# Rebuilding the linear-attention half of a fused attention kernel, and giving its scheduler a model of side-by-side row tiles

## The chip, the cores and the metric

The kernel runs on one core of a Trainium2 chip. The time is the duration of one execution on the device in microseconds (us). Times below are medians of several executions; a ratio is the mean time of one kernel's fast runs over that of the other's fast runs of the same rounds, so it is not quite the ratio of the medians quoted beside it. Each run also reports the share of the full TensorE clock that was granted. Runs that took over 1.5% more than the fastest of their kernel in the same job are called slow and are left out of means and ratios.

## The reference

The program computes two independent attention layers on sequences of 2048 rows, with model width 512 and 32 heads of 16, and puts their outputs side by side.

```python
# A: softmax attention, 32 query heads share one key head and one value head
q = (x @ wq) as (32, 2048, 16);  k = x @ wk;  v = x @ wv        # k, v: (2048, 16)
a = concat_heads(softmax(q @ k.T / 4) @ v) @ wo
# B: linear attention, per head
q, k, v = split(x @ wqkv)
phi(u) = [softmax(u @ w_phi), softmax(-(u @ w_phi))]            # 16 + 16 features
kv = phi(k).T @ v;   z = sum over rows of phi(k)
b = concat_heads(phi(q) @ kv / (phi(q) @ z + 1e-6)) @ wo
out = concat([a, b], axis=-1)
```

## The kernel before

Part A is a stream of 2048 score tiles, each 128 keys by 512 queries of one head. A score matmul needs only 16 of its 32 rows of weights, so four heads sit on four row tiles (partitions 0, 32, 64, 96) of TensorE. Each tile has to be exponentiated. ACT does that for two or three tiles in one instruction (`L1616` in the profile). DVE does it with a bit trick: it writes the bits of a float16 with one multiply-add from PSUM (`L1708`), makes three shifted copies for four tiles at once (`L1721`), and PE sums the four with weights (`L1746`). Four such tiles are called a group here.

A list scheduler, written in Python and run while the program is built, decides how many groups DVE takes and in which order everything is issued. It keeps a clock for each engine; B's work is spread between A's. The order is fixed before the chip sees it (a check at the end falls back to a general version for inputs out of range; these inputs do not need it). The parts that the argument touches:

```python
def issue(self, j, start):              # the scheduler books job j on its engine
    dur = j.dur
    if j.eng == "pe" and j.mode != self.mode:
        dur += self.SWITCH              # changing between full, row and column tiling
        self.mode = j.mode
    self.te[j.eng] = start + dur        # PE is taken until then, whatever row tile it was
    ...

def next_dq(self):                      # offers the next score tile of a DVE group
    ...
    g = next((x for x in self.dleft if x not in self.busy), self.dleft[0])   # its row tile
    ...
    self.job(("dq", k), "pe", 0.22, scores, mode="row", nb=1, prio=1.0, ok=self.dq_ok)

# in run(): put matmuls on zeros ("fills") into a gap of PE, to keep its clock up
gap = s - te - ...
if n >= 2 and te > 14 and self.active(s) < self.ACTIVE:
    ...
```

B works row by row: project q and k transposed, copy them out of PSUM, multiply by `w_phi`, exponentiate into float32, normalise each feature, and only then use it:

```python
# per 128 rows, 32 times (16 for keys, 16 for queries)
ssum = reduce_add(epn, per head and sign)               # L1976, DVE
bmx = max(ssum, bmx);  rs = 1 / ssum                    # L1982, L1983, DVE
phi = epn * rs                                          # L1991, DVE, 128x1024
# keys: kv += phi.T @ [v, 1]
# queries: transpose phi on PE, copy out, multiply by kv and z, divide
den = ps[..., 64:68] + 1e-6;  rden = 1 / den            # L2067, L2069, DVE
o_sb = ps[..., 0:64] * rden                             # L2070, DVE
# transpose o, copy out, multiply by wo, copy out, store
```

## Time and profile before

The median was 853.77 us when the prediction was made (847.48 to 860.23). The profiled run took 863.85 us at a clock of 0.925. The first lines come from the profile page of the kernel before: the span, the busy time of each engine with its share of the span and its number of instructions, the granted clock in 40 slices (in tenths), and the chain of work that ended last, by engine.

```profile
span 862.1 us, 17064 instructions
## 1 busy us (share of the span) xinstructions
PE 785.0 (91%) x7214; PEld 252.0 (29%) x7278; DVE 728.3 (84%) x1286; ACT 777.2 (90%) x714; POOL 14.7 (2%) x46
...
## 2 busy tenths in 40 slices
...
PEclk9779979889999999998999999978979999699998
...
## 4 chain that ended last, share of the span: by engine, by line
DVE 53%; PE 30%; ACT 12%; DMA 2%; issue 2%; SPq 1%; DVEq 0%; POOL 0%; POOLq 0%
```

Three engines are close together: PE 91%, ACT 90%, DVE 84%. The clock row has five slices at 7 and one at 6. The next lines are groups of instructions by line of the kernel; after the bar stand busy us and mean ns of one, then the idle time of the engine just before them and what ended it.

```profile
## 5 line engine op out<-in xcount | busy, mean ns | idle before, releaser
L1616 ACT ACTIVATE f_PT<-f_ps 128x1536 bf16<-128x1536 f32 (+1 forms) x645 | 747.7, 1263 | 65.4 <-PE f_ps L1561 60.1
L1561 PE MATMUL f_ps<-f_QA,f_KR 32*128 32x512 bf16 x2048 | 348.9, 407 | 35.6 <-ACT f_PT L1616 11.8
L1708 DVE TENSOR_SCALAR f_Z<-f_ps 128x512 int16<-128x512 f32 x436 | 283.3, 679 | 41.3 <-PE f_ps L1561 39.9
L1721 DVE TENSOR_SCALAR f_Z<-f_Z 128x2048 int16<-128x2048 int16 x327 | 213.2, 681 | 0.9
...
L1378 PE MATMUL f_ps<-f_ones,f_zero 128*128 128x512 bf16 (+7 forms) x274 | 84.6, 385 | 2.1 <-POOL f_zero L1397 1.3
...
L1976 DVE TENSOR_REDUCE f_ssum<-f_epn 128x64 f32<-128x1024 f32 x32 | 38.6, 1205 | 2.6 <-ACT f_epn L1970 2.6
L1991 DVE TENSOR_TENSOR f_phi<-f_epn,f_rs 128x1024 bf16<-128x1024 f32 x32 | 38.7, 1210 | 0.1
```

ACT had 1612 tiles (2048 less 436) in 747.7 us, 0.464 us each. DVE had 436 tiles, 109 groups, in 283.3 + 213.2 us, 4.56 us per group. `L1378` are the fills. ACT waited 60.1 us for score matmuls. `L1976` and `L1991` are two of the linear part's DVE instructions; all of the linear part's DVE groups add up to about 194 us.

Two lines of the timeline of the kernel before (start us, duration us, engine, instruction) show what row tiles do on the chip:

```profile
start us, us, engine line op out<-in xcount [idle before <-releaser]
...
830.91 0.38 PE L1561 MATMUL f_ps<-f_QA,f_KR 32*128 32x512 bf16 x1
...
833.84 0.39 PE L1561 MATMUL f_ps<-f_QA,f_KR 32*128 32x512 bf16 x3
```

One score matmul keeps PE busy for 0.38 us, three on different row tiles for 0.39 us. The Trainium skill says the same in "TensorE: Matmul & The Clock Gate", Part 3 on packing: matmuls on different row groups run concurrently. The scheduler knew it for the two or three tiles that it issues as one job for ACT, but not for the single tiles it issues for DVE: each of those took 0.22 us of its PE clock even when it ran beside others.

### The profile page before, as it was taken

The page shows a single profiled execution, that of the slowest core. Times are in us where ns is not written, and L with a number is a line of the kernel's source. Part 1 is how long each engine was busy: PE and PEld are TensorE (multiplying, and loading weights), DVE is VectorE, ACT ScalarE, POOL GpSimd, SP SyncE. Part 2 cuts the span into 40 slices and gives each one's busy share as a digit, 9 for nine tenths or more (in the row PEclk, how much of TensorE's full clock was granted, in tenths as well). Part 3 has the DMA queues.
Part 4 walks back from the last instruction along what each step waited for, and adds up shares of the span by engine and source line. Part 5 has one row for each costly group of instructions (what it writes and reads, how often), then busy time and mean ns, then how long its engine had stood idle before and what let it go on. Part 6 is the DMA issues. An engine that isn't in the chain of part 4 may idle for free.

```text
span 862.1 us, 17064 instructions
## 1 busy us (share of the span) xinstructions
PE 785.0 (91%) x7214; PEld 252.0 (29%) x7278; DVE 728.3 (84%) x1286; ACT 777.2 (90%) x714; POOL 14.7 (2%) x46
## 2 busy tenths in 40 slices
PE   8989999999999999999899888999999999998894
PEld 2222223223323333322233333332333332222231
DVE  4778989998956999989996889998989778799942
ACT  4879989999999999999999999989899999799972
POOL 5000000000000000001000000000000000000000
PEclk9779979889999999998999999978979999699998
DMA  6841001111101111100111101110111110111110
GB/s 127 182 44 8 5 5 8 7 8 8 8 7 27 8 8 8 8 4 6 8 7 30 22 8 13 20 13 8 13 13 21 20 27 19 7 8 7 7 8 28
DMA packets 40922, 17.08 MB, mean 20 GB/s; under 512 B 32836, under 2 KB 38468, under 8 KB 40840
## 3 DMA queue, kind: packets, MB, share of 16 engines
q1 hardware_dynamic: 40840, 15.93, 14.8%
q8 instruction: 59, 0.97, 0.5%
q14 instruction: 23, 0.19, 0.1%
HBM read 3.19 MB, written 4.19 MB: 9 GB/s over the span
## 4 chain that ended last, share of the span: by engine, by line
DVE 53%; PE 30%; ACT 12%; DMA 2%; issue 2%; SPq 1%; DVEq 0%; POOL 0%; POOLq 0%
DVE f_Z L1708 18%; DVE f_Z L1721 14%; ACT f_PT L1616 12%; PE f_ps L1561 11%; PE f_ps L1658 5%; PE f_ps L1746 5%; DVE f_phi L1991 3%; DVE f_ssum L1976 3%; PE f_ps L1378 3%; PE f_ps L1929 2%; DVE f_accS L1384 2%; DVE f_o_sb L2070 1%; DVE f_rs L1983 1%; PE f_ps L1802 1%; DVE f_On L1789 1%
## 5 line engine op out<-in xcount | busy, mean ns | idle before, releaser
L1616 ACT ACTIVATE f_PT<-f_ps 128x1536 bf16<-128x1536 f32 (+1 forms) x645 | 747.7, 1263 | 65.4 <-PE f_ps L1561 60.1
L1561 PE MATMUL f_ps<-f_QA,f_KR 32*128 32x512 bf16 x2048 | 348.9, 407 | 35.6 <-ACT f_PT L1616 11.8
L1708 DVE TENSOR_SCALAR f_Z<-f_ps 128x512 int16<-128x512 f32 x436 | 283.3, 679 | 41.3 <-PE f_ps L1561 39.9
L1721 DVE TENSOR_SCALAR f_Z<-f_Z 128x2048 int16<-128x2048 int16 x327 | 213.2, 681 | 0.9
L1658 PE MATMUL f_ps<-f_PT,f_VA 128*32 128x512 bf16 x1612 | 169.3, 411 | 2.9 <-DVE f_accS L1384 2.8
L1561 PEld LDWEIGHTS f_ps<-f_QA,f_KR 32*128 32x128 bf16 x2048 | 82.9, 92 | 273.6 <-ACT f_PT L1616 100.7
L1746 PE MATMUL f_ps<-f_Z,f_VK 128*32 128x512 f16 x1744 | 123.6, 407 | 4.7 <-DVE f_Z L1721 2.1
L1378 PE MATMUL f_ps<-f_ones,f_zero 128*128 128x512 bf16 (+7 forms) x274 | 84.6, 385 | 2.1 <-POOL f_zero L1397 1.3
L1658 PEld LDWEIGHTS f_ps<-f_PT,f_VA 128*32 128x32 bf16 x1612 | 41.5, 93 | 120.1 <-issue 107.0
L1746 PEld LDWEIGHTS f_ps<-f_Z,f_VK 128*32 128x32 bf16 x1744 | 40.1, 100 | 61.6 <-issue 18.5
L1976 DVE TENSOR_REDUCE f_ssum<-f_epn 128x64 f32<-128x1024 f32 x32 | 38.6, 1205 | 2.6 <-ACT f_epn L1970 2.6
L1991 DVE TENSOR_TENSOR f_phi<-f_epn,f_rs 128x1024 bf16<-128x1024 f32 x32 | 38.7, 1210 | 0.1
L1929 PE MATMUL f_ps<-f_BxT,f_Bw 128*128 128x512 bf16 x111 | 33.3, 420 | 4.4 <-issue 2.3
L1970 ACT ACTIVATE f_epn<-f_ps 128x512 f32<-128x512 f32 x64 | 35.5, 626 | 1.8 <-PE f_ps L1961 1.6
L1378 PEld LDWEIGHTS f_ps<-f_ones,f_zero 128*128 128x128 bf16 (+2 forms) x274 | 21.4, 100 | 41.2 <-issue 28.9
L1384 DVE CAST f_qkT<-f_ps 128x512 bf16<-128x512 f32 x32 | 21.9, 685 | 9.7 <-PE f_ps L1929 9.5
L1789 DVE TENSOR_TENSOR f_On<-f_accS,f_denS 128x512 bf16<-128x512 f32 x31 | 21.1, 681 | 4.3 <-DMA f_denS<-f_denS 4.2
L1802 PE MATMUL f_ps<-f_wo_pad,f_On 128*128 128x512 bf16 x87 | 22.9, 381 | 2.1 <-issue 1.0
L1384 DVE COPY f_accS<-f_ps 128x512 f32<-128x512 f32 x31 | 21.1, 682 | 4.0 <-PE f_ps L1658 3.0
L1384 DVE CAST f_outA<-f_ps 128x512 bf16<-128x512 f32 x12 | 8.3, 690 | 18.5 <-PE f_ps L1802 18.5
L1513 DVE TENSOR_SCALAR f_KR<-f_ps,f_half 128x512 bf16<-128x512 f32 x8 | 5.6, 745 | 15.2 <-PE f_ps L1505 15.2
L1983 DVE RECIPROCAL f_rs<-f_ssum 128x64 f32<-128x64 f32 x32 | 17.4, 544 | 0.0
(83 smaller groups left out, 326.2 us busy)
## 6 DMA issues: line engine op xcount, KB each, us to landing
f_denS<-f_denS SPq DMA_DIRECT2D x124, 30.0 KB, 3.1
out_dram<-f_outB SPq DMA_DIRECT2D x16, 128.0 KB, 1.7
f_denC<-f_accS SPq DMA_DIRECT2D x124, 2.0 KB, 1.7
f_denS<-f_denC SPq DMA_DIRECT2D x124, 2.0 KB, 1.7
f_Bw<-in_B_wqkv_dram SPq DMA_DIRECT2D x1, 1536.0 KB, 7.4
out_dram<-f_outA SPq DMA_DIRECT2D x6, 256.0 KB, 2.3
f_wq<-in_A_wq_dram SPq DMA_DIRECT2D x1, 512.0 KB, 4.0
f_Bwo<-in_B_wo_dram SPq DMA_DIRECT2D x1, 512.0 KB, 10.1
```

The source lines that it names most:

```text
L1378: mm = pe.matmul(ps[0:m, bank, 0:n].rearrange("p (a n) -> p a n", n=128), lhsT=zero[0:r, 0:m], rhs=rhs, start=start, stop=start, **kw)
L1384: self.add("dve", lambda v: v.tensor_copy(out=out, in_=in_), reads=reads, writes=writes)
L1561: return pe.matmul(self.ps[:, bank, :], lhsT=self.KR[32 * g:32 * g + 32, sc % 2, kap * 128:(kap + 1) * 128], rhs=self.QA[32 * g:32 * g + 3 ...
L1616: self.add("act", lambda a: a.activation(out=PT[:, sl[0]:sl[0] + size, :], in_=ps[:, b0:b0 + size, :], func=ACT.Exp), reads=[("PS", b0 + i ...
L1658: mm = pe.matmul(ps[32 * g:32 * g + 32, bank, :], lhsT=w, rhs=PT[:, slots[g], :], start=start, stop=stop, tile_position=(0, 32 * g))
L1708: self.add("dve", lambda v: v.tensor_scalar(out=o, in0=ps[:, bank, :], scalar1=self.Z1, scalar2=self.Z0, op0=ALU.mult, op1=ALU.add), reads ...
L1721: self.add("dve", lambda v: v.tensor_scalar(out=Z[:, t], in0=Z[:, 0], scalar1=256.0 * t, scalar2=None, op0=ALU.add), reads=zk, writes=[("Z ...
L1746: mm = pe.matmul(ps[32 * g:32 * g + 32, bank, :], lhsT=w[:, k, :], rhs=Zf[:, k, sl[g], :], start=start and k == 0, stop=stop and k == 3, t ...
L1929: mm = pe.matmul(ps[:, bank, :], lhsT=w[:, dc, col0:col0 + 128], rhs=xT[:, dc, sck * 512:(sck + 1) * 512], start=(dc == 0), stop=(dc == 3))
L1970: self.add("act", (lambda a, sg: (lambda e: e.activation(out=epn[:, a, :], in_=ps[:, bank, :], func=ACT.Exp, scale=sg)))(a, sg), reads=[(" ...
L1976: self.add("dve", lambda v: v.tensor_reduce(out=ssum[:, r, :], in_=epn.rearrange("p a (h f) -> p (a h) f", h=32), axis=AX.X, op=ALU.add), ...
L1991: self.add("dve", lambda g: g.tensor_tensor(out=o, in0=i0, in1=i1, op=ALU.mult), reads=["epn", "epn2", ("rs", r)], writes=[("phi", pr)])
```

## The change

The linear part is rebuilt to use less DVE time. `wk @ w_phi` and `wq @ w_phi` are multiplied once on the chip, so features come straight from x. The key features stay unnormalised; the values are multiplied by the reciprocal sums instead, half as many rows of work as before. The query features are computed already transposed, for both signs, are never normalised, and their sums enter through a small matmul and one weight per head, sign and row.

```diff
+mm = pe.matmul(ps[...], lhsT=wT[:, 4 * w + c, ...], rhs=wphi[:, c, :], ...)   # fuse weights, once
-phi = epn * rs                        # 32 times 128x1024
+vS[:, :, :, 0:16] = v3 * rs           # 16 times 128x1024, keys only
+vS[:, :, :, 16:17] = rs
-tr: pe.transpose(phi)  ->  copy       # queries: transpose after the exponent
+b_pq: matmul(lhsT=Wq (both signs), rhs=xT), 512 columns;  ET = exp(ps)   # features on partitions
+b_qs: 32 small matmuls per 512 rows give both sums of each head; b_qw: weights from them
+o_sb[:, a] = ps[:, a] * w             # 32 times 128x512, both signs, added by the transpose on PE
```

The scheduler gets a clock for each row tile:

```diff
-        self.te[j.eng] = start + dur
+        if j.mode == "row" and j.name[0] in ("qk", "dq"):
+            ...
+            self.row_free = start + dur - j.dur + 0.02
+            for x in tiles:
+                self.tile_end[x] = start + dur
+        self.te[j.eng] = max(self.te[j.eng], start + dur)
...
+    def pe_from(self, j, te):          # from when PE can take j
+        if j.mode != "row" or self.mode != "row" or j.name[0] not in ("qk", "dq"):
+            return te
+        tiles = [self.dq_tile(self.row_free)] if j.name[0] == "dq" else self.row_tiles[j.name[1]]
+        return max([self.row_free] + [self.tile_end[g] for g in tiles])
```

And settings move: the ring of exponentiated tiles `RING` from 15 to 20, `HIGH` from 9 to 13 (how far value matmuls may lag), `AGE` from 5 to 3, the fill threshold `ACTIVE` from 5.8 to 6.4, the end of the stretch for B from 700 to 600. Fills may now also use a free PSUM bank, and some output buffers and the last output products are laid out anew.

## The prediction

> **What bounds the kernel now.** The work is one pool of 2048 score tiles (32 sub-rows x 512), exponentiated either by ACT or, by a bit trick, by DVE in groups of four. The page's busy table shows PE 91%, ACT 90% (777 us), DVE 84% (728 us) of the 862.1 us span. The groups by line give 1612 tiles to ACT (747.7 us, 0.464 us each) and 436 = 109 groups of four to DVE (283.3 + 213.2 us, 4.56 us per group). The rest of DVE, about 232 us, is copies and the linear part. So ACT and DVE together are the bound and PE is close behind; DVE time taken from the linear part is worth something only because the list scheduler refills it with score tiles. The chain that ended last agrees: DVE 53%, PE 30%, ACT 12%.
>
> **DVE removed (groups by form).** Linear part before: sums 38.6, phi 38.7, reciprocal 17.4, running max 6.8, q/k copies 21.9, v 10.8, transposed phi 10.9, den/rden/o 26.7, oT 6.5, outB 10.9, kv 4.7: about 194 us.
> **DVE added (estimates from the same durations).** Weight copies 12 x 0.68 = 8; key sums 16 x 1.2 = 19; reciprocal and max 16 x 0.76 = 12; values divided by sums 16 x 1.4 = 22; kv adds 7; query weights 4 x 2.9 = 11.5; scaled outputs 32 x 0.68 = 22; oT and outB 22: about 124 us. The skill page "VectorE: DVE Perf Modes" (perf-mode tier table) has tensor_reduce at 1x only, so bf16 features do not make the sum cheaper than the 1.205 us of now. Net saving about 70 us, 65 after overlap.
> **ACT:** 64 exps of 128x512 before and after (35.5 us): no change.
> **PE:** projections grow from 128 to 192 matmuls of 512 columns (+14 us), kv and transposes about even; each group moved to DVE needs 16 instead of 4 value matmuls (about +0.65 us). PE gets about 20-25 us more real work, but 84.6 us of it now are clock-keeping fills on zeros, so most is absorbed.
>
> **Critical share.** A balance: ACT busy share x T = 29.5 + 0.464 x (2048 - 4n), DVE share x T = other + 4.556 n, n groups. It returns 862 for before. With other = 165 and unchanged shares (90.1%, 84.5%) T = 841 (-2.5%). So of 65 us about 21 reach the time.
> **Scheduler.** Idle before ACT exps is 65 us (60 from score matmuls), before DVE's first step 41 us (40 likewise). In the timeline three row tiles take 0.39 us, as one does; the skill page "TensorE: Matmul & The Clock Gate" (Part 3, packing) says disjoint row groups run concurrently. The old model books 0.22 us of PE for each. With the new one and a ring of 20 instead of 15 I expect ACT near 91.5%, DVE near 87%: another 10-20 us. The tail (about 30 us after 830 with ACT half idle) shrinks by 1-3 us. Clock: 0.925 granted, but ACT is busy 91% in slow and in full-clock windows alike, so more fills buy little.
>
> Predicted: **824 us**, range 803 to 846; faster by over 2%: 0.76, within 2%: 0.20, slower: 0.04.
>
> **Right if:** DVE's linear lines sum to 115-135 us; DVE groups rise from 109 to 116-128 and ACT tiles fall to about 1540-1585; ACT's wait on score matmuls falls below 50 us; DVE busy stays 84-89%.
> **Wrong if:** DVE goes idle instead of taking groups, because banks are held longer (values wait for the sums in PSUM, four query-weight banks) or PE cannot feed it: then DVE falls below 82%, groups stay near 109 and time stays within 2%. Or PE saturates (over 95%). If the row-tile model alone removes most waits, time may be below 805.

## The result, and the profile after

The changed kernel took 814.96 us (809.98 to 815.92, 4 runs) beside 852.72 us of the kernel before (4 runs). The ratio is 0.9566 with a 95% interval of 0.9511 to 0.9621. One of the four runs of the kernel before, 860.23 us, is slow and not in the ratio. Predicted were 824 us with a range of 803 to 846. The same lines of the page after:

```profile
span 806.9 us, 17313 instructions
## 1 busy us (share of the span) xinstructions
PE 733.9 (91%) x7345; PEld 243.7 (30%) x7420; DVE 722.3 (90%) x1254; ACT 748.5 (93%) x690; POOL 16.7 (2%) x49
...
PEclk9788999999999999999999998999999999999997
...
## 4 chain that ended last, share of the span: by engine, by line
DVE 63%; PE 25%; DMA 5%; ACT 2%; SPq 2%; issue 2%; DVEq 0%
```

```profile
L1653 ACT ACTIVATE f_PT<-f_ps 128x1536 bf16<-128x1536 f32 (+1 forms) x621 | 721.4, 1264 | 45.3 <-PE f_ps L1598 42.1
L1745 DVE TENSOR_SCALAR f_Z<-f_ps 128x512 int16<-128x512 f32 x496 | 324.1, 682 | 34.9 <-PE f_ps L1598 34.3
L1598 PE MATMUL f_ps<-f_QA,f_KR 32*128 32x512 bf16 x2048 | 315.6, 390 | 31.1 <-DVE f_Z L1745 20.8
L1758 DVE TENSOR_SCALAR f_Z<-f_Z 128x2048 int16<-128x2048 int16 x372 | 244.5, 685 | 0.7
...
L1404 PE MATMUL f_ps<-f_ones,f_zero 128*128 128x512 bf16 (+7 forms) x204 | 61.2, 361 | 2.1 <-POOL f_zero L1423 1.3
...
L2152 DVE TENSOR_TENSOR f_Wk<-f_ps,f_wq 128x512 bf16<-128x512 f32 x32 | 21.9, 684 | 3.0 <-PE f_ps L2141 2.9
...
L2041 DVE TENSOR_TENSOR f_vS<-f_ps,f_rs 128x1024 bf16<-128x1024 f32 x16 | 19.5, 1220 | 1.2 <-PE f_ps L2031 1.1
...
L2015 DVE TENSOR_REDUCE f_ssum<-f_Ek 128x64 f32<-128x1024 bf16 x16 | 19.4, 1214 | 0.1
```

The groups of four on DVE rose from 109 to 124 (496 tiles), ACT's tiles fell from 1612 to 1552, its wait for score matmuls from 60.1 to 42.1 us, and its busy time from 777.2 to 748.5 us. Of the 55.2 us between the two profiled spans, 28.7 us are less work of ACT and 26.5 us less idle time of ACT. The 60 tiles that moved, at 0.464 us each, explain the first part: 27.8 us. The second part is smaller in usual runs: the trace before is of a slow run and the trace after of the fastest of its kernel, and the means of the fast runs (below) are only 41.8 us apart, which leaves about 14 us for it. The clock row is full almost everywhere. The windows from 60 to 760 us, first before and then after, give busy us (and instructions) of PE, PEld, DVE, ACT and POOL, then the granted clock, the DMA share and GB/s:

```profile
60.00:760.00 700.00, 648.87 (x6046) 212.09 (x6104) 618.58 (x1090) 658.30 (x609) 3.86 (x9) 0.93 0.12 12
```

```profile
60.00:760.00 700.00, 652.16 (x6648) 219.18 (x6716) 663.56 (x1140) 680.95 (x630) 4.83 (x10) 0.99 0.13 12
```

ACT went from 94.0% to 97.3% busy in this stretch, DVE from 88.4% to 94.8%, and the clock from 0.93 to 0.99.

### The profile page after: what moved, and what is told of

Read it like the earlier page. It is cut to its first block, busy times and chain, and to the rows that moved or that the text cites. A ratio compares the mean times of both kernels' runs of the same rounds, so it can differ in the third digit from the quotient of the medians.

```text
span 806.9 us, 17313 instructions
## 1 busy us (share of the span) xinstructions
PE 733.9 (91%) x7345; PEld 243.7 (30%) x7420; DVE 722.3 (90%) x1254; ACT 748.5 (93%) x690; POOL 16.7 (2%) x49
## 4 chain that ended last, share of the span: by engine, by line
DVE 63%; PE 25%; DMA 5%; ACT 2%; SPq 2%; issue 2%; DVEq 0%
DVE f_Z L1745 27%; DVE f_Z L1758 19%; PE f_ps L1598 8%; PE f_ps L1783 5%; PE f_ps L1695 4%; DMA f_AxT<-in_A_x_dram 2%; DVE f_vS L2041 2%; PE f_ps L2092 2%; ACT f_PT L1653 2%; DVE f_ssum L2015 2%; DVE f_accS L1410 2%; DMA f_BxT<-in_B_x_dram 2%; DVE f_On L1826 2%; PE f_ps L1839 2%; DVE f_Wk L2152 2%
## 5 line engine op out<-in xcount | busy, mean ns | idle before, releaser
L1653 ACT ACTIVATE f_PT<-f_ps 128x1536 bf16<-128x1536 f32 (+1 forms) x621 | 721.4, 1264 | 45.3 <-PE f_ps L1598 42.1
L1745 DVE TENSOR_SCALAR f_Z<-f_ps 128x512 int16<-128x512 f32 x496 | 324.1, 682 | 34.9 <-PE f_ps L1598 34.3
L1598 PE MATMUL f_ps<-f_QA,f_KR 32*128 32x512 bf16 x2048 | 315.6, 390 | 31.1 <-DVE f_Z L1745 20.8
L1758 DVE TENSOR_SCALAR f_Z<-f_Z 128x2048 int16<-128x2048 int16 x372 | 244.5, 685 | 0.7
L1404 PE MATMUL f_ps<-f_ones,f_zero 128*128 128x512 bf16 (+7 forms) x204 | 61.2, 361 | 2.1 <-POOL f_zero L1423 1.3
L2092 PE MATMUL f_ps<-f_BxT,f_Wq 128*128 128x512 bf16 x112 | 29.4, 380 | 3.3 <-issue 1.6
L2152 DVE TENSOR_TENSOR f_Wk<-f_ps,f_wq 128x512 bf16<-128x512 f32 x32 | 21.9, 684 | 3.0 <-PE f_ps L2141 2.9
L2041 DVE TENSOR_TENSOR f_vS<-f_ps,f_rs 128x1024 bf16<-128x1024 f32 x16 | 19.5, 1220 | 1.2 <-PE f_ps L2031 1.1
L2099 ACT ACTIVATE f_ET<-f_ps 128x512 bf16<-128x512 f32 x32 | 20.2, 636 | 0.4 <-PE f_ps L2092 0.4
L2015 DVE TENSOR_REDUCE f_ssum<-f_Ek 128x64 f32<-128x1024 bf16 x16 | 19.4, 1214 | 0.1
```

The costliest lines, as they stand in the source:

```text
L1404: mm = pe.matmul(ps[0:m, bank, 0:n].rearrange("p (a n) -> p a n", n=128), lhsT=zero[0:r, 0:m], rhs=rhs, start=start, stop=start, **kw)
L1598: return pe.matmul(self.ps[:, bank, :], lhsT=self.KR[32 * g:32 * g + 32, sc % 2, kap * 128:(kap + 1) * 128], rhs=self.QA[32 * g:32 * g + 3 ...
L1653: self.add("act", lambda a: a.activation(out=PT[:, sl[0]:sl[0] + size, :], in_=ps[:, b0:b0 + size, :], func=ACT.Exp), reads=[("PS", b0 + i ...
L1745: self.add("dve", lambda v: v.tensor_scalar(out=o, in0=ps[:, bank, :], scalar1=self.Z1, scalar2=self.Z0, op0=ALU.mult, op1=ALU.add), reads ...
L1758: self.add("dve", lambda v: v.tensor_scalar(out=Z[:, t], in0=Z[:, 0], scalar1=256.0 * t, scalar2=None, op0=ALU.add), reads=zk, writes=[("Z ...
L2092: mm = pe.matmul(ps[:, bank, :], lhsT=w[:, dc].rearrange("p x h a f -> p (x h a f)")[:, G * 128:G * 128 + 128], rhs=xT[:, dc, m * 512:(m + ...
```

## The experiments

Twelve kernels were run, four at a time on one chip beside the kernel before, with five rounds each. All gave correct results. "Clock" is the mean of the fast runs. The kernel before took 855.9 us on average over 24 fast runs of these three jobs, at a mean clock of 0.943. The changed kernel in its own job: 814.1 us over five runs, clock 0.969.

| run | linear part | row model | settings | groups | mean us | ratio (95%) | clock |
|---|---|---|---|---|---|---|---|
| before | old | old | old | 109 | 855.9 | 1 | 0.943 |
| e1 | old | new | old | 115 | 838.8 | 0.982 (0.976 to 0.988) | 0.965 |
| e2 | new | old | old | 109 | 838.9 | 0.980 (0.972 to 0.987) | 0.960 |
| e3 | new | old | new | 113 | 826.8 | 0.971 (0.964 to 0.978) | 0.967 |
| e4 | new | new | old | 121 | 828.4 | 0.971 (0.966 to 0.976) | 0.964 |
| after | new | new | new | 124 | 814.1 | 0.957 (0.951 to 0.962) | 0.969 |
| e5 | new, 70 us DVE added | new | new | 116 | 832.7 | 0.970 (0.967 to 0.974) | 0.964 |
| e6 | new | new | new, no fills | 123 | 823.8 | 0.960 (0.956 to 0.963) | 0.926 |
| e7 | old | old | old, more fills | 111 | 850.8 | 0.991 (0.987 to 0.996) | 0.952 |
| e8 | new | new | new, AGE 3.1 | 121 | 815.4 | 0.950 (0.947 to 0.954) | 0.976 |
| e9 | new | new | new, ring 15 | 124 | 813.4 | 0.949 (0.945 to 0.953) | 0.968 |
| e10 | old | old | searched | 114 | 845.1 | 0.987 (0.981 to 0.993) | 0.955 |
| e11 | new | new | searched | 125 | 808.1 | 0.943 (0.939 to 0.947) | 0.978 |
| e12 | new, A's products on POOL | new | searched | 125 | 827.9 | 0.965 (0.960 to 0.969) | 0.954 |

The changed kernel has 0.957 in its own job, and 0.949 in e9, whose instructions come in the same order. Ratios of different jobs are therefore good to about 0.8%; differences below are taken inside a job where they can be.

### e1 to e4: the parts one by one

e1 is the kernel before with the scheduler's diff above and nothing else. e2 is the changed kernel with that diff and the settings undone; "linear part new" in the table therefore also holds the other edits of the change (fills in free banks, output buffers and their order), which no run takes apart:

```diff
-        tiles = [...]                      # e2, e3: pe_from
-        return max([self.row_free] + ...)
+        return te
-        self.te[j.eng] = max(self.te[j.eng], start + dur)
+        self.te[j.eng] = start + dur
-    RING = 20;  HIGH = 13;  AGE = 3.0;  ACTIVE = 6.4;  T_B = (54.0, 600.0)     # e2, e4
+    RING = 15;  HIGH = 9;  AGE = 5.0;  ACTIVE = 5.8;  T_B = (54.0, 700.0)
```

> Kernel before with only the scheduler's new row-tile model; linear part, ring of 15 and settings as before. The program built has 115 DVE groups (before: 109). Theory 1 (mine: two gains that add, linear rebuild about -2.5% and scheduler with its settings -1 to -2.5%): 0.980 to 0.990 of before. Theory 2 (the two need each other; DVE is already 84% busy with the old linear part, so the better model alone finds little free DVE time): 0.985 to 1.00. ACT's wait on score matmuls falls from 60 us under both.

> New linear part with the old row-tile model and the old settings (ring 15, HIGH 9, AGE 5, ACTIVE 5.8, linear part spread to 700). Theory 1: the freed 65 us of DVE are refilled with score groups, about 118 groups, 0.975 of before. Theory 2: the old model books PE time for each score tile that the chip does not spend, so the scheduler does not offer the freed DVE time to score groups; the built program has 109 groups as before, DVE busy falls to about 660 us (80%), and the time falls only by what shorter waits give: 0.985 to 1.00.

> The changed kernel with the old row-tile model, new settings kept (built: 113 groups instead of 124). Theory 1: 0.965 to 0.975 of before (loses 1 to 2%). Theory 2: 0.975 to 0.99 of before, DVE busy about 670 us, so most of the gain is gone though DVE's linear work is as small as in the changed kernel.

> The changed kernel with its settings back (ring 15, HIGH 9, AGE 5, ACTIVE 5.8, linear part to 700), row-tile model and linear part new (built: 121 groups). Both theories: small loss against the changed kernel, 0.960 to 0.975 of before. If settings were the main thing: above 0.98.

Each part alone gave about 16 us in this job (854.6 us before): e1 0.982, e2 0.980. Added to the other, each gave about 10 us more (e4: 828.4), and the settings another 12 to 14 (e2 to e3; e4 to the changed kernel, across jobs). So the three add up, nearly. The rival, that the two need each other, fits the times less well: e1, e2 and e3 lie below its ranges (0.985 to 1.00 for the first two, 0.975 to 0.99 for e3), though all three intervals just reach into them. But its mechanism was half right. The page of e2, where the linear part alone is new:

```profile
span 841.0 us, 16959 instructions
...
PE 774.4 (92%) x7249; PEld 243.8 (29%) x7249; DVE 669.9 (80%) x1149; ACT 774.3 (92%) x714; POOL 16.3 (2%) x49
...
L1653 ACT ACTIVATE f_PT<-f_ps 128x1536 bf16<-128x1536 f32 (+1 forms) x645 | 748.2, 1275 | 53.0 <-PE f_ps L1597 50.0
...
L1745 DVE TENSOR_SCALAR f_Z<-f_ps 128x512 int16<-128x512 f32 x436 | 285.5, 684 | 69.0 <-PE f_ps L1597 67.9
```

No group moved: still 436 tiles on DVE, DVE fell to 80% busy as the rival said, and DVE's wait for score matmuls rose to 67.9 us. Yet ACT's waits fell: ACT is idle for 66.7 us (841.0 less 774.3), 84.9 before. So freed DVE time seems to pay without being refilled. In the table of waits of e2, the two PE queues together wait for DVE 147 us, 185 us before (sums of all such lines): PE, whose program is one fixed order, stands less long before instructions that need DVE, and so reaches ACT's score matmuls earlier (its waits for ACT rose from 121 to 139 us). That is a reading of the waits, not shown by a run of its own. The clock is a rival for much of it: from 60 us to 40 us before the end, the stretches of half clock that begin there add up to 51 us in e2 and to 102 us in the trace before. At the price found below, 23 us for 99 us, that is about 12 of the 18 us; by the mean clocks of this job (0.947 and 0.960), and 3.6 us per 0.01, it is about 5 of the 16 us.

### e5: 70 us of DVE work put back

```diff
+for i in range(58):
+    fn = lambda: self.add("dve", lambda v: v.tensor_reduce(out=scr, in_=src, axis=AX.X, op=ALU.add), ...)
+    self.job(("xx", i), "dve", 1.14, fn, prio=1.9, rel=70.0 + 11.0 * i)
```

> The changed kernel plus 58 useless DVE sums of 1.2 us (70 us, about what the linear rebuild saved), known to the scheduler, spread over 70 to 700 us, writing a scratch tile. The program built has 116 groups instead of 124. Theory 1 (the linear rebuild pays through DVE time that is refilled with score groups; the balance of the prediction gives 22 us for 70 us of DVE): 0.978 to 0.988 of before. Rival (it pays through fewer PSUM bank turns and shorter chains, not through DVE time): 0.957 to 0.968, nearly the changed kernel.

The measured ratio, 0.970, lies between both ranges, because the changed kernel itself was better in this job (0.950 for its twin e8) than in the one that the ranges were built on. Against that twin the 58 sums cost 17.3 us (832.7 less 815.4), where the balance gave 22 and the rival nothing. ACT's work accounts for about 9 us of that (five groups fewer than e8, 20 tiles at 0.464 us), and the clock, lower by 0.012, for about 4 at the rate found below. So DVE time is at least a large part of what the linear rebuild pays with, and 1 us of it is worth about 0.25 us in this kernel, not the 0.31 of the prediction's balance.

### e6 and e7: the fills and the clock

Both change `ACTIVE` alone, to 0 in the changed kernel (e6) and from 5.8 to 6.4 in the kernel before (e7).

> The changed kernel without the fill matmuls after the head (threshold ACTIVE 0 instead of 6.4; built: 123 groups instead of 124, other settings the same). Theory C (the granted clock is worth time: 11 runs of the kernel before that differ in nothing else give 4.75 us per 0.01 of clock): clock falls from 0.97 to 0.93 or less and the time rises by 20 us or more, 0.975 to 1.0 of before. Rival, as the prediction had it (the clock buys little): 0.955 to 0.965. If the clock stays above 0.96 without fills, the fills are not what keeps it.

> Kernel before with only the fill threshold of the changed kernel (ACTIVE 6.4 instead of 5.8; built: 111 groups instead of 109). Theory C1 (more fills raise the clock): clock from 0.937 to 0.955 or more, 0.985 to 0.992 of before. Theory C2 (the clock rose because the new row-tile model made the real work denser and saw the gaps, as in the run with that model alone, which had 0.965 with fewer fills): clock below 0.95, 0.992 to 1.002.

Without fills the clock fell to 0.926, and the page of e6 shows it in many slices:

```profile
span 822.3 us, 16848 instructions
...
PE 730.4 (89%) x7115; PEld 233.0 (28%) x7190; DVE 722.1 (88%) x1247; ACT 751.2 (91%) x692; POOL 16.6 (2%) x49
...
PEclk8586996997889999999999999899999999997998
```

The time rose by 8.4 us against the twin e8 in the same job. That is more than the jog of e8 moved, and less than the 20 us expected from the clock; the fills' own PE time, about 70 us in e8, came free at the same moment. In e7 the clock rose from 0.941 to 0.952 with more fills: the time fell by 0.9%, inside theory C1's range and just outside C2's, though the clock rose a little less than C1 wanted. The row model alone (e1) raised the clock more, to 0.965, with fewer fills: 73.3 us against 84.6 us. So fills hold the clock, but more fill time is not why it rose in the changed kernel, which has less of it (61.2 us). It rose with each part alone: to 0.965 in e1 and to 0.960 in e2, from 0.947 in that job. Which property of the order does it (denser scores, or gaps that the old model did not see and so did not fill) was not separated.

### e8 to e12: luck, ring, settings and a further step

```diff
-    AGE = 3.0
+    AGE = 3.1                                        # e8
-    RING = 20
+    RING = 15                                        # e9
+    AHEAD = 5; AGE = 2.0; HIGH = 11; DBUSY = 4.2; T_B = (54.0, 600.0); ACTIVE = 6.4      # e10, on the kernel before
+    AHEAD = 4; AGE = 4.0; HIGH = 15; T_B = (54.0, 540.0); ACTIVE = 5.8                   # e11, on the changed kernel
-    job(("on", sc), "dve", 0.60, ...);   self.add("dve", ... tensor_tensor(out=On ...))
+    job(("on", sc), "pool", 1.80, ...);  self.add("pool", ... tensor_tensor(out=On ...)) # e12, settings searched again
```

> The changed kernel with one meaningless step of a setting (AGE 3.1 instead of 3.0), which reshuffles the order of the greedy scheduler: a measure of how much of any difference is the luck of one order (built: 121 groups instead of 124). Expected 0.957 to 0.968 of before; differences of up to 1% between variants are then not to be read as causes.

> The changed kernel with its ring of exponentiated tiles back at 15 and nothing else (the built order of instructions is the same as with 20, so this is also the changed kernel once more beside the runs below). If the slots of the ring are waited for on the chip: ACT gains waits on value matmuls and 0.96 to 0.97 of before. If not, as the scheduler's plan has it: the ratio of the changed kernel, 0.950 to 0.962.

> Kernel before with settings alone re-tuned (the best of 100 random settings by the scheduler's own plan: AHEAD 5, AGE 2, HIGH 11, DBUSY 4.2, linear part to 600, ACTIVE 6.4; built: 114 groups instead of 109). If re-tuning is a large part of the change's gain: 0.975 to 0.985 of before. If it is only luck of the order: 0.985 to 1.0.

> The changed kernel with the best of 600 random settings by the scheduler's own plan (plan 0.1% shorter, 125 groups). Expected equal to the changed kernel within 1%: 0.947 to 0.962 of before. Clearly under 0.945 would mean that settings still hold something.

> The changed kernel with the 31 products of the attention outputs with their reciprocal sums (0.68 us each, 21 us of DVE) on the idle POOL engine, with settings searched again (built: 125 groups). Theory 1 (DVE time is worth about a quarter of itself, as the 70 us put back cost 17.5 us): 5 us less, 0.944 to 0.956 of before. Rival (PE with its mode switches is the bound now, more free DVE time buys nothing; or POOL and DVE disturb each other): 0.95 to 0.965.

e8 moved three groups back to ACT and came out at 0.950, below its expected range as the changed kernel itself did in these jobs (e9: 0.949). Its mean is 2.0 us (0.2%) above e9, in another job, so this reshuffled order moved the time little, though one jog is a small sample. e9, at 813.4 us, gave the time of the changed kernel (814.1): the larger ring buys nothing. e10 shows what re-tuning alone is worth to the old kernel: 1.3%. Its ratio fell in the range set for luck, at its better end, but the difference is far over the jog of e8, so I read it as a small gain of tuning: a quarter to a third of the change's 4.3 to 5.1%. That goes against the reading set beforehand, and one order cannot exclude luck. e11, below its expected range too, beats both kernels: 806.12 to 809.70 us, where e9 has 810.92 to 814.83 in the same job, and a clock of 0.978.

e12 missed the range of theory 1 (0.944 to 0.956) and came out at the end of the rival's (0.965). It took 21 us off DVE and was 14.5 us slower than e9, at a clock of 0.954. Two lines of its groups, and then one line each of e12 and e9 for the three shifted copies, which give the shortest, median and longest duration in ns:

```profile
L1758 DVE TENSOR_SCALAR f_Z<-f_Z 128x2048 int16<-128x2048 int16 x375 | 257.6, 712 | 0.8
...
L1826 POOL TENSOR_TENSOR f_On<-f_accS,f_denS 128x512 bf16<-128x512 f32 x31 | 43.8, 1411 | 718.8 <-DMA f_denS<-f_denS 718.7
```

```profile
L1758 DVE TENSOR_SCALAR f_Z<-f_Z x375: 622/683/1765, 31.7 to 790.7; 128x2048 int16<-128x2048 int16 x188
```

```profile
L1758 DVE TENSOR_SCALAR f_Z<-f_Z x372: 627/684/884, 31.6 to 790.8; 128x2048 int16<-128x2048 int16 x186
```

The products took 1411 ns on POOL. In the trace 38 of the 375 shifts overlap one of them, and 13 of these 38 took 1160 to 1765 ns; no other shift of e12, and none of e9, took over 1000 ns. All 13 began while a product was running and ended 0.55 us after it; the shifts that began first kept their 0.68 us, and the products that ran beside them often took 1.4 to 1.8 us instead of 1.27. So it looks as if the later of the two waits for the earlier, unless it begins when the earlier is nearly done. The Trainium skill's "GPSIMD Engine Reference", in the table of its specifications, has the SBUF interfaces shared with VectorE, with contention where DVE runs in a 2-port mode or reads two SBUF inputs; this trace agrees that they contend, but does not show in which mode the shifts ran. The stretched shifts add about 11 us of DVE time (their durations less 0.684 us each) and arrive at moments that the fixed order did not plan for. How much of the loss is that and how much the clock stays open.

## Why the prediction was right, and where it was not

**Bound and balance.** Right. ACT and DVE share the score tiles and PE is close behind. DVE's linear groups after add up to 126 us (weights 7.7, sums 19.4, reciprocals and maximum 12.3, values 24.4, kv 7.0, query weights 11.6, outputs 21.9, oT and outB 21.9); 124 were predicted from the durations of the kernel before. The sum of bf16 features took 1.214 us, of float32 ones 1.205 us: as the tier table of the skill's "VectorE: DVE Perf Modes" has it, tensor_reduce gains nothing from bf16. Groups rose to 124 (116 to 128 predicted), ACT tiles fell to 1552 (1540 to 1585), ACT's wait to 42.1 us (below 50). DVE's busy share, 90%, went just over the 84 to 89% predicted.

**What DVE time is worth.** Somewhat too high. The balance gave 21 us for the linear rebuild. e2 has 16 us for it alone, e1 to e4 has 10 us on top of the row model, and e5 charges 17 us for putting 70 us back, where the balance charged 22. The balance holds the busy shares still, and it lets DVE time pay only through moved tiles; e2 paid without moving one.

**Scheduler.** Too low as a whole: 10 to 20 us were predicted for the row model and the ring together. The row model alone gave 16 (e1), 10 on top of the new linear part (e2 to e4), and the settings another 12 to 14. The ring, named in the prediction, gave nothing (e9). Two errors of opposite sign met. The rest of the distance from 824 to 815 is mostly the starting point: the prediction took about 38 us off the slow profiled run (span 862.1), the change took 41.8 us off the mean of the fast runs (855.9).

**The clock: the step that failed.** The prediction said: "ACT is busy 91% in slow and in full-clock windows alike, so more fills buy little." The windows behind that sentence had been placed wrongly: the clock's records count from the start of the recording, 11 us before the span begins, and I had read them as counted from the span. Placed rightly, the matmuls of `L1929` that start in stretches of half clock have a median of 0.634 us and the others 0.379 us; placed as before, both have 0.379 us. The kernel before shows this in its stretches of half clock from 64.5 to 818.9 us (columns as in the windows above; the last line is the sum of all 13 stretches), and then the sum of its stretches at full clock:

```profile
core 0: us, PE busy (x) PEld busy (x) DVE busy (x) ACT busy (x) POOL busy (x), PEclk, DMA share, GB/s
112.33:122.57 10.24, 9.91 (x47) 2.34 (x47) 7.72 (x14) 7.20 (x7) 0.00 (x0) 0.50 0.01 2
166.94:177.18 10.24, 10.24 (x104) 2.53 (x100) 8.71 (x16) 7.19 (x7) 0.00 (x0) 0.50 0.02 2
...
736.97:754.04 17.07, 16.53 (x102) 3.63 (x102) 11.90 (x20) 12.21 (x11) 0.00 (x0) 0.50 0.07 5
...
sum 98.98, PE 97.16 PEld 24.74 DVE 78.15 ACT 73.37 POOL 0.78; mean PE 7.47 PEld 1.90 DVE 6.01 ACT 5.64 POOL 0.06
```

```profile
sum 655.37, PE 600.06 PEld 201.35 DVE 592.44 ACT 638.20 POOL 3.08; mean PE 42.86 PEld 14.38 DVE 42.32 ACT 45.59 POOL 0.22
```

At half clock ACT is busy 73.37 of 98.98 us, 74%; at full clock 638.20 of 655.37, 97%. That costs 98.98 x 0.974 - 73.37 = 23 us in this run. In e9, the same order of instructions as the changed kernel, the sums from 65.6 to 587.9 us are, at half and at full clock (after that and up to 40 us before the end all is at full clock):

```profile
sum 30.73, PE 29.47 PEld 6.78 DVE 25.51 ACT 22.16 POOL 0.00; mean PE 5.89 PEld 1.36 DVE 5.10 ACT 4.43 POOL 0.00
```

```profile
sum 491.51, PE 457.33 PEld 153.60 DVE 465.14 ACT 482.07 POOL 4.84; mean PE 91.47 PEld 30.72 DVE 93.03 ACT 96.41 POOL 0.97
```

There 30.73 us are left, and they cost 30.73 x 0.981 - 22.16 = 8 us. Both are estimates: they put all of ACT's extra idle time in these stretches down to the clock. The runs of the kernel before that differ in nothing but chance say the same: over its 24 fast runs time and clock go together (correlation -0.77) at 3.6 us per 0.01 of clock. From a mean clock of 0.943 to 0.969 that is 9 us, about a fifth of the 42 us between the means. The slow runs lie on the same line; over all 33 runs it is 5.0 us per 0.01 (correlation -0.91), which would make 13 us. So the clock looks like a real part of the gain, smaller than the moved tiles (28 us) and not the main one; no run changes it alone. The conclusion of the failed sentence was less wrong than its reason: more fills bought 0.9% in e7, and no fills cost 8.4 us in e6.

**PE.** Its share stayed at 91%, not saturated by this measure. Fill time fell from 84.6 to 61.2 us, about as much as the 20 to 25 us of new PE work that the prediction counted, which fits its "most is absorbed"; no run separates the two.

## What to carry to other kernels

When two engines share one pool of work under a fixed order, time saved on one of them is worth a fraction of itself (a quarter here), and part of it may arrive as shorter waits, not as moved work. Before crediting a rewrite, re-tune the old version and jog a meaningless setting: here tuning alone was worth about 1.3% to the old kernel (interval 0.7 to 1.9%), and one jog moved 0.2%. Put every record on one time axis before comparing, and check it on something that must line up, such as matmuls that take longer where the clock is low.

## What the Trainium skill lacked or had wrong

- "TensorE: Matmul & The Clock Gate" ("Why this matters for your kernels": no idle gaps over about 3 us between bursts keep the clock up). Here the clock fell to half 12 times between 60 and 760 us in the kernel before although PE's longest gap between matmuls in that stretch was 0.89 us; PE was busy 70 to 91% of the 3.4 us before each drop. Avoiding long gaps was not enough for this stream of small tiles, and the page gives no figure for how busy PE has to be instead.
- The same page's note that the throttle ratio is binary (Part 1) agrees with this one-core kernel: all records of these traces are 0.5 or 1, in stretches that are multiples of 3.41 us (but for the last of a trace, which is cut off). What it lacks is what half clock costs a kernel that PE only feeds: ACT's busy share fell from 97% to 74%.
- No page read here says how far the granted clock varies between executions of one program on one core: 0.918 to 0.960 in the runs of the kernel before, fast and slow, over three jobs, with times of 847 to 873 us.
